# The written-out opening of a two-branch kernel in a new order: an own norm root for each of the first two blocks, the first unit's products block by block

## The chip, the cores and the metric

The kernel runs on one core of one Trainium2 chip. The metric is the device time of one execution in microseconds; lower is better. Before the change it is 443.17 us (median of 3 runs, 442.64 to 443.61).

## The reference

`x` has 2048 rows of 448 numbers. A layer norm is followed by two branches whose results are added to `x`:

```python
xn = _layernorm(x, axis=-1)                      # (x - mean) / sqrt(var + 1e-5)
X  = rfft2(xn, axes=(-2, -1)) * (w_r + 1j * w_i) # spectral branch
a  = irfft2(X, s=(2048, 448))
gate, up = xn @ W_gate, xn @ W_up                # 448 -> 1792
b  = (relu(gate) * up) @ W_down                  # 1792 -> 448
out = x + a + b
```

## The kernel before, in words

Everything stays in one core's memory. Rows of `x` lie in 16 blocks of 128; block n2 belongs to slab q = n2 % 4 at place j = n2 // 4, so a slab is 512 rows. Slabs are worked in the order 0, 2, 1, 3. The 1792 columns of the gate and up weights are 14 tiles f of 128; the two halves of a tile are g0 (gate) and g1 (up). A unit (f, q) is the products of both halves of tile f with slab q. To keep the accuracy of float32, each operand is split into two float16 numbers, hi and lo (the residual); the products are hi x hi, lo x hi and hi x lo. In the code these are three parts of one list: the first three of seq1 (hi weights, hi data), the last three of seq1 (lo weights, hi data), and seq2 (hi weights, and data of the tail tiles, mostly lo).

A block of a slab goes through these steps. SP issues its load (`lx`, load_xr, L225; block 4 comes with the identity for the transposes in one load, L220). VectorE takes its statistics (`st`, ln_stats, L255 and L258). ScalarE takes a first reciprocal root (`sq`, ln_sd, L266) and VectorE improves it by one Newton step (`rs`, ln_rstd, L271 to L275). The normalised block is formed on VectorE (`xn`, L297) or ScalarE (`ax`, L295), its float16 hi on ScalarE (`hi`, `hx`, L304 or L306), two small tail copies on GpSimd (`cp`, L310 and L311), and the residual lo on VectorE (`lo`, ln_lo, L321 and L322). For slab 0 TensorE then transposes the eight tiles (`tpA` the three hi tiles, `tpB` the others, L337), and ScalarE or VectorE copies the result out of PSUM into T (`aev`, `vev`, L345). For the other slabs a transposing DMA does both (`dm`, ln_dma, L330); slab 2's four transfers are the first of these.

A weight half goes: load (`lw`, L231), squares summed on ScalarE (`wsq`, L185), sum over partitions on GpSimd (`par`, L188), a power of two from it on VectorE (`wsc`, L191 and L195), hi on ScalarE (`whi`, L699), lo on VectorE (`wlo`, L703). After a unit, ScalarE and VectorE take turns: `re` (relu, L799), `tm` (gate times up, L803), `gh` (hi, L807), `gl` (lo, L811). `wdq`, `wdp`, `wdsc`, `wdh` and `wdl` prepare the down projection's weights; its products are on L834.

The opening, from the start to the first two units of slab 2, is one string, OPENING. Each word is a piece, and the pieces issue their instructions in the order of the string:

```python
with tc.manual_schedule(engines={PE, DVE, Activation, SP, Pool}):   # names shortened
    A.activation(mt([128, 1], F32, "root"), eps, AF.Abs_reciprocal_sqrt)
    V.memset(warm, 0.0)
    wps = banks[2][0]
    gu_open(0, q)
    for name in OPENING.split():
        pieces[name]()
```

Each engine runs its own instructions strictly in this order; nothing moves an instruction past another of the same engine. So the string sets five rows at once, one for each engine, SP's row of transfers among them. `warm` issues products of a zeroed tile into an unused bank (L1094), `kw4` four more. In the opening, the products of unit (0, slab 0) and (1, slab 0) stand in pieces by half of the slab (256 columns: `hh`, `lh`, `hl` for tile 0, `ah`, `bh`, `ch` for tile 1, followed by the half g and the slab half); later units are whole (`gu`, 512 columns). `hp` is the half-height pass that closes a pair of units (L764). `gz0` and `gz1` are the first two units of slab 2: their first product reads all four blocks of the slab. `n0` gathers the ninth tile of slab 0 by four small transfers. Behind the opening, a scheduler orders the rest of the program.

Of the kernel before, what the change touches and what calls it, by code (L numbers as in the profile page):

```python
# [10 lines left out]
F32 = mybir.dt.float32  # L11
# [3 lines left out]
OP = mybir.AluOpType  # L15
# [10 lines left out]
NWARM = 21  # L26
# [3 lines left out]
OPENING = """lx0 st0 lx4 st4 sqA rsA ax4 hi0 lx8 st8 lx12 xn0 lw cp0 lw lw lw hx4 warm tpA4 st12 tpA0 lo0 lx6 sqB rsB cp4 lo4  # L30
wsqW0g0 tpB0 kw4 tpB4 wsqW0g1 lx2 hi8 parW0g0 wscW0g0 lwd1 whiW0g0 vevA0 parW0g1 wscW0g1 vevA4 hh00 tpA8 whiW0g1
ly4 hi12 lw hh10 lw lw lw wsqW1g1 wsqW1g0 vevB4 vevB0 hl00 wloW0g0 parW1 wloW0g1 tpA12 vevA12 hl10 vevA8 lh00
cp8 xn8 lh10 hh11 lw ax12 lh11 wscW1 whiW1g0 hh01 cp12 whiW1g1 lh01 lw lo8 wsqW2g1 wsqW2g0 tpB8 ah00 lwd0 lo12
tpB12 wsqW3g0 vevB8 wloW1g0 ah10 wsqW3g1 vevB12 ah01 parW2 ah11 lwd2 wloW1g1 wscW2 bh00 hl11 hl01 lx14 whiW2g0
bh01 hp0 ch10 whiW2g1 lw st2 bh11 st6 re0 wloW2g0 bh10 wsqW4g1 ch00 ch11 tm0 gu2g0 parW3 wscW3 st14 wsqW4g0
whiW3g0 wloW2g1 ch01 ly0 parW4 wscW4 whiW3g1 wloW3g1 lw wsqW5g1 lx10 whiW4g0 wloW3g0 gh0 re1 st10 gu2g1 tm1 hp2
sqC rsC wsqW5g0 xn6 gu3g0 re2 parW5 wscW5 whiW5g0 tm2 wloW4g0 xn10 xn14 hx14 lwd4 hx6 lo6 hi10 whiW5g1 lo10
gu4g0 hx2 wloW5g0 whiW4g1 cp14 xn2 wdq0 gl0 cp10 gu3g1 wloW4g1 lo14 lwd3 wdq4 wdq2 cp2 re3 tm3 cp6 wloW5g1 gh1
gu4g1 gh2 wdq3 ly12 lo2 hp4 wdq1 wdp wdsc wdh4 dm10 gl1 re4 ly8 wdh3 gl2 gu5g1 tm4 gh4 dm14 gl4 dm6 gu5g0 dm2
re5 lfd gz0g0 wdl3 gz0g1 tm5 hp6 gh3 gl3 rz0 gh5 wdl4 gl5 wdh1 wdl1 wdh2 wdl2 n0 wdh0 wdl0 gz1g0 tz0 gz1g1 rz1  # L40
hz0 tz1 hz1 lz0 lz1
# [103 lines left out]
def tile_gfnet_reglu(ctx: ExitStack, tc: tile.TileContext, x, xr, xi, wgu, wd, wf, c_fd, c_fm, c_im, c_row, c_id,  # L145
# [106 lines left out]
    def ln_stats(q, j):  # L252
        n2 = q + 4 * j
        st = ft([128, 6], F32, "bst", 2)
        V.bn_stats(st, xr_t[n2])  # L255
        if j == 0:
            mv[q] = ft([128, 4, 2], F32, "mv", 2)
        V.bn_aggr(mv[q][:, j, :], st)  # L258

    rst = {}  # L260

    def ln_sd(q, js=(0, 1, 2, 3)):
        w = ft([128, 4, 4], F32, "rs", 3)
        n = len(js)
        rst[q, js[0]] = w[:, :, 0:n], mv[q][:, js[0]:js[-1] + 1, :]
        A.activation(w[:, 0, 0:n], rst[q, js[0]][1][:, :, 1], AF.Abs_reciprocal_sqrt, bias=eps)  # L266

    def ln_rstd(q, js=(0, 1, 2, 3), bias=False):
        w, m = rst[q, js[0]]
        r0, t, r, nm = (w[:, i] for i in range(4))  # L270
        V.scalar_tensor_tensor(t, m[:, :, 1], 1e-5, r0, op0=OP.add, op1=OP.mult)  # L271
        V.scalar_tensor_tensor(t, t, -0.5 * 2048, r0, op0=OP.mult, op1=OP.mult)
# [17 lines left out]
    def ln_xn(n2, act=False):  # L290
        xn_b[n2] = free.pop(0)
        xn[n2] = xn_b[n2].rearrange("p g c k -> p (g c k)")[:, 0:D]
        r, nm, mean = rst[n2 % 4, n2 // 4]
        if act:
            A.activation(xn[n2], xr_t[n2], AF.Identity, scale=r, bias=nm)  # L295
        else:
            V.tensor_scalar(xn[n2], xr_t[n2], mean, r, op0=OP.subtract, op1=OP.mult)  # L297

    def ln_hi(n2, fused=False):
        new_tt(n2)  # L300
        o = tt[n2].rearrange("p a b -> p (a b)")[:, 0:D]
        r, nm, _ = rst[n2 % 4, n2 // 4]
        if fused:
            A.activation(o, xr_t[n2], AF.Identity, scale=r, bias=nm)  # L304
        else:
            A.activation(o, xn[n2], AF.Copy)  # L306
# [12 lines left out]
    def ln_lo(n2):  # L319
        x, t = xn[n2], tt[n2].rearrange("p a b -> p (a b)")  # L320
        V.tensor_tensor(t[:, 512:896], x[:, 0:384], t[:, 0:384], op=OP.subtract)  # L321
        V.tensor_tensor(t[:, 448:512], x[:, 384:448], t[:, 384:448], op=OP.subtract)  # L322
        free.append(xn_b.pop(n2))
# [373 lines left out]
    def w_hi(f, g):  # L697
        w = wt[f, g] = mt([128, 8, 128], F16, "wt", 2 * NR + 4)
        A.activation(w[:, 0:4, :], wst[f, g], AF.Copy, scale=wsc[f, g])  # L699
# [392 lines left out]
    def keep_warm(n):  # L1092
        for _ in range(n):
# [3 lines left out]
              "lw": load_wn, "warm": lambda: keep_warm(NWARM),  # L1097
              **{f"kw{n}": (lambda n=n: keep_warm(n)) for n in (1, 3, 4)},
# [6 lines left out]
    for c, q in enumerate(CHUNKS[:2]):  # L1105
# [31 lines left out]
    for f in groups[0] + [ahead[2]]:  # L1137
# [149 lines left out]
```

## Time and profile before

| what | value |
|---|---|
| time, median of 3 | 443.17 us |
| profiled execution, span | 440.9 us |
| TensorE (PE) busy | 435.7 us, 99% |
| VectorE (DVE) busy | 382.3 us, 87% |
| ScalarE (ACT) busy | 184.5 us, 42% |
| DMA | 39.55 MB, mean 90 GB/s |

The profile is one profiled execution; its times are microseconds from the start of the span. What lies around the span is the difference to the device time, 443.17 - 440.9 = 2.3 us by the median. A busy TensorE says little, since products overlap in the records; what it waited for, and at what moment, says more. Lines such as L757 are line numbers of the kernel before. In a row of the timeline the columns are start, length, engine, line, operation, what is written and read, shape and count, and in brackets the idle time before it with what ended it.

### The profile page before, as it was taken

The numbers are of one execution on the slowest core, as the hardware profiler recorded it, in microseconds if no ns is written. First come the engines' busy times: TensorE is split into PE (matmuls) and PEld (weight loads), VectorE is DVE, ScalarE is ACT, GpSimd is POOL, SyncE is SP. The second block draws the span as 40 slices with busy tenths as digits, with TensorE's granted clock in tenths as the row PEclk, the third lists the DMA queues.
The fourth block names the chain that finished last, engine by engine and source line by source line (L and its number), as shares of the span: only waits on it lengthen the run. The fifth ranks groups of instructions, "written<-read, shape, count | busy, mean of one in ns | idle before, by whom it ended". The sixth has DMA issues, their size and how long they took to land.

```text
span 440.9 us, 7429 instructions
## 1 busy us (share of the span) xinstructions
PE 435.7 (99%) x2641; PEld 221.9 (50%) x2641; DVE 382.3 (87%) x957; ACT 184.5 (42%) x396; POOL 29.4 (7%) x75
## 2 busy tenths in 40 slices
PE   8999999999999999999999999999999999999996
PEld 3744464554445545444545444444545555555664
DVE  6998496989887879999999999988997989798644
ACT  6995427392457236144023467233113332243220
POOL 3230002011100040000000020000000000000000
PEclk9999999999999999999999999999999999999999
DMA  7929895304111123332220210001111121210212
GB/s 256 301 91 198 269 364 172 70 2 107 59 49 50 47 76 119 94 118 84 86 84 1 84 43 1 0 1 42 44 43 49 54 91 34 72 55 33 89 51 104
DMA packets 37613, 39.55 MB, mean 90 GB/s; under 512 B 16535, under 2 KB 33353, under 8 KB 37577
## 3 DMA queue, kind: packets, MB, share of 16 engines
q1 hardware_dynamic: 37576, 39.09, 29.1%
q8 instruction: 20, 0.33, 0.3%
q14 instruction: 17, 0.13, 0.1%
HBM read 24.38 MB, written 3.67 MB: 64 GB/s over the span
## 4 chain that ended last, share of the span: by engine, by line
PE 90%; DVE 4%; ACT 3%; DMA 1%; issue 1%; SPq 0%; POOL 0%; ACTq 0%
PE bank L757 49%; PE bank L834 27%; PE bank L764 3%; PE fx L648 2%; PE fx L369 2%; PE fx L667 2%; PE fx L406 2%; PE bank L853 2%; ACT wt L699 1%; DMA T<-tt 1%; ACT junk L185 1%; DVE bst L255 1%; DVE wt L703 1%; DMA y<-in_xr 1%; ACT tt L304 1%
## 5 line engine op out<-in xcount | busy, mean ns | idle before, releaser
L757 PE MATMUL bank<-T,wt 128*128 128x512 f16 (+1 forms) x1160 | 252.7, 372 | 0.6 <-DVE T L345 0.5
L757 PEld LDWEIGHTS <-wt 128*128 128x128 f16 x1160 | 110.9, 98 | 127.6 <-issue 7.2
L834 PE MATMUL bank<-wdt,h 128*128 128x448 f16 x624 | 122.4, 352 | 0.0
L834 PEld LDWEIGHTS <-h 128*128 128x128 f16 x624 | 60.5, 98 | 55.1
L799 ACT ACTIVATE g<-bank 128x512 f32<-128x512 f32 x56 | 33.0, 591 | 80.4 <-PE bank L757 45.2
L807 ACT ACTIVATE h<-g 128x512 f16<-128x512 f32 x56 | 35.0, 627 | 70.1 <-DVE g L803 70.0
L803 DVE SCALAR_TENSOR_TENSOR g<-bank,g 128x512 f32<-128x512 f32 x56 | 38.2, 683 | 11.9 <-PE bank L757 6.8
L811 DVE TENSOR_TENSOR h<-g,h 128x512 f16<-128x512 f32 x56 | 38.1, 684 | 6.7 <-ACT h L807 6.4
L840 DVE SCALAR_TENSOR_TENSOR xy<-bank,dsc,xy 128x448 f32<-128x448 f32 x44 | 29.8, 676 | 5.5 <-PE bank L834 5.2
L632 ACT ACTIVATE vt<-y,fsc 128x456 f16<-128x456 f32 x15 | 10.1, 674 | 34.5 <-issue 14.0
L699 ACT ACTIVATE wt<-wst,wsc 128x512 f16<-128x512 f32 x28 | 19.3, 713 | 11.1 <-DVE wsc L195 10.3
L703 DVE SCALAR_TENSOR_TENSOR wt<-wst,wsc,wt 128x512 f16<-128x512 f32 x28 | 20.4, 742 | 0.5 <-ACT wt L699 0.3
L672 DVE SCALAR_TENSOR_TENSOR xy<-fx,fsc,xy 128x448 f32<-128x448 f32 x16 | 10.8, 680 | 10.9 <-PE fx L667 10.9
L188 POOL PARTITION_ALL_REDUCE wm<-wm x15 | 10.5, 697 | 139.9 <-ACT junk L185 136.4
L185 ACT ACTIVATE junk<-wst 128x512 bf16<-128x512 f32 x28 | 17.2, 616 | 0.0
L397 ACT ACTIVATE Xh<-X 128x456 f16<-128x456 f32 x16 | 9.3, 579 | 16.4 <-DVE X L395 9.3
L764 PE MATMUL bank<-T,wt 64*128 64x512 f16 x112 | 15.6, 380 | 0.0
L400 DVE TENSOR_TENSOR Xh<-X,Xh 128x456 f16<-128x456 f32 x16 | 9.8, 624 | 4.9 <-ACT Xh L397 4.9
L648 PE MATMUL fx<-im,vt 128*128 128x128 f16 x192 | 13.3, 219 | 0.0
L667 PEld LDWEIGHTS <-pgh 114*128 114x128 f16 x192 | 10.9, 98 | 3.8 <-issue 0.8
L648 PEld LDWEIGHTS <-vt 128*128 128x128 f16 x192 | 11.6, 98 | 1.3
L406 PE MATMUL fx<-Xh,fm 128*128 128x456 f16 x48 | 12.2, 356 | 0.0
(168 smaller groups left out, 480.1 us busy)
## 6 DMA issues: line engine op xcount, KB each, us to landing
wst<-in_wgu SPq DMA_DIRECT2D x28, 256.0 KB
sw<-y SPq DMA_DIRECT2D x56, 112.2 KB
wf<-in_wf SPq DMA_DIRECT2D x16, 228.0 KB
xy<-in_x SPq DMA_DIRECT2D x16, 224.0 KB
y<-in_xr SPq DMA_DIRECT2D x15, 224.0 KB
out<-xy SPq DMA_DIRECT2D x15, 224.0 KB
wdst<-in_wd SPq DMA_DIRECT2D x14, 224.0 KB
fm<-in_c_fm SPq DMA_DIRECT2D x4, 256.0 KB
```

What stands on the lines that cost most here:

```text
L185: A.activation(mt([128, 512], BF16, "junk", 2)[:, 0:src.shape[-1]], src, AF.Square, scale=SQ, accum_out=acc)
L648: P.matmul(o, v[:, h, w], m[:, c, :], start=(i == 0), stop=(i == 2), skip_group_check=True)
L699: A.activation(w[:, 0:4, :], wst[f, g], AF.Copy, scale=wsc[f, g])
L703: V.scalar_tensor_tensor(w[:, 4:8, :], st, sc, w[:, 0:4, :], op0=OP.mult, op1=OP.subtract)
L757: last["P"] = P.matmul(hps[f, q][g][:, cs], wt[f, g][:, a, :], Tq[q][:, b, cs], start=(start and i == 0), stop=(stop and i == len(seq) - 1 ...
L764: m = P.matmul(hps[f, q][g][:, 0:512], wt[f, g][rows, 7, :], Tq[q][rows, b, :], start=start, stop=stop).ins
L799: last["A"] = A.activation(g1s[f, q], hps[f, q][0], AF.Relu, scale=2.0 ** -22).ins
L803: last["V"] = V.scalar_tensor_tensor(g1, hps[f, q][1], 2.0 ** -22, g1, op0=OP.mult, op1=OP.mult).ins
L807: A.activation(ht[f, q][:, 0, :], g1s[f, q], AF.Copy)
L811: V.tensor_tensor(h[:, 1, :], g1s.pop((f, q)), h[:, 0, :], op=OP.subtract)
L834: last["P"] = P.matmul(ps[:, 0:D], ht[f, q][:, a, js], wdt[f][:, b, :], start=(i == 0), stop=(i == n - 1)).ins
L840: last["V"] = V.scalar_tensor_tensor(xy[:, n2, :], dps[n2][:, 0:D], dsc[:, g:g + 1], xy[:, n2, :], op0=OP.mult, op1=OP.add).ins
```

## The change

OPENING is another string. In words, what it does in the first microseconds: the load of block 4 is issued ahead of that of block 0, both halves of weight tile 0 come third and fourth, and blocks 8 and 12 fifth and eighth. Blocks 4 and 0 each have an own root and an own Newton step (`sq4 rs4`, `sq0 rs0`) instead of one for both; their bias is no longer formed there but later (`nm0`, `nm4`). Block 4 is normalised on VectorE instead of ScalarE. The hi copies of both (`hx4`, `hx0`) come from the normalised block. The warm-up has 14 products instead of 21. Tile 0's products with the first half of slab 0 are split by block: `hq`, `lq` and `kq`, followed by the half g and the block's place j, take 128 columns each. The first group of copies out of PSUM (the hi tiles of blocks 0, 4 and 8) is ScalarE's (`aevA`) instead of VectorE's.

The core of the diff:

```diff
-OPENING = """lx0 st0 lx4 st4 sqA rsA ax4 hi0 lx8 st8 lx12 xn0 lw cp0 lw lw lw hx4 warm tpA4 st12 tpA0 lo0 lx6 sqB rsB cp4 lo4
-wsqW0g0 tpB0 kw4 tpB4 wsqW0g1 lx2 hi8 parW0g0 wscW0g0 lwd1 whiW0g0 vevA0 parW0g1 wscW0g1 vevA4 hh00 tpA8 whiW0g1
...
+OPENING = """lx4 warm14 lx0 st4 lw sq4 st0 wsqW0g0 rs4 lw parW0g0 sq0 lx8 lw wsqW0g1 kw4 xn4 rs0 hx4 wscW0g0 whiW0g0 lw xn0 parW0g1
+hx0 cp4 st8 wscW0g1 wsqW1g0 cp0 tpA0 tpA4 wsqW1g1 aevA0 lx12 lo0 whiW0g1 tpB0 hq00 aevA4 lo4 vevB0 st12 parW1 tpB4
...
     def ln_sd(q, js=(0, 1, 2, 3)):
-        w = ft([128, 4, 4], F32, "rs", 3)
+        w = ft([128, 4, 4], F32, "rs", 4)
...
         if bias:
-            V.scalar_tensor_tensor(nm, m[:, :, 0], -1.0, r, op0=OP.mult, op1=OP.mult)
+            ln_bias(q, js)
...
+    def ln_bias(q, js):
+        w, m = rsb[q, js[0]]
+        V.scalar_tensor_tensor(w[:, 3], m[:, :, 0], -1.0, w[:, 2], op0=OP.mult, op1=OP.mult)
...
+            piece(f"sq{n2}", ln_sd, q, (j,))
+            piece(f"rs{n2}", ln_rstd, q, (j,))
+            piece(f"nm{n2}", ln_bias, q, (j,))
...
             if f == 0:
+                for j in range(2):
+                    for tag, sq in (("hq", seq1[0:3]), ("lq", seq1[3:6]), ("kq", seq2)):
+                        piece(f"{tag}{g}{j}", gu_full, f, q, (g,), slice(128 * j, 128 * j + 128), tag == "hq" and j == 0,
+                              False, sq)
```

Further new pieces (`px`, `ph`, `pl`, `vh`, `pw`, `vw`) move steps to GpSimd or VectorE; the string does not use them.

How rows of engines move, at three places. First SP's row at the start. In it `g1` is block 4 with the identity, the other `y` are blocks of slab 0 or 2 in the order of the string, and `wst` are weight halves. Before:

```order
L225 DMA y0_66<-in_xr 128x448
L220 DMA g1_127<-in_xi 128x512
L225 DMA y2_68<-in_xr 128x448
L225 DMA y3_69<-in_xr 128x448
L231 DMA wst_146<-in_wgu 128x512
L231 DMA wst_150<-in_wgu 128x512
L231 DMA wst_152<-in_wgu 128x512
L231 DMA wst_154<-in_wgu 128x512
```

And now:

```order
L219 DMA g1_122<-in_xi 128x512
L224 DMA y0_66<-in_xr 128x448
L230 DMA wst_143<-in_wgu 128x512
L230 DMA wst_156<-in_wgu 128x512
L224 DMA y1_67<-in_xr 128x448
L230 DMA wst_162<-in_wgu 128x512
L230 DMA wst_180<-in_wgu 128x512
L224 DMA y4_70<-in_xr 128x448
```

Tile 0's two halves moved from the fifth and sixth place to the third and fourth, block 8 from third to fifth, block 12 from fourth to eighth.

Second, VectorE's row from the second but last residual of slab 2 on. `tt` are the blocks in float16: before, tt0 is block 14 and tt3 block 2. Rows that write `g1` are `tm`, those that write `h` are `gl`, those that write `wt` are `wlo`. Before:

```order
L811 TENSOR_TENSOR h_465<-g1_404,h_465 128x512
L703 SCALAR_TENSOR_TENSOR wt_541<-wst_315,wsc_450,wt_541 128x512
L321 TENSOR_TENSOR tt0_100<-y13_79,tt0_100 128x384
L322 TENSOR_TENSOR tt0_100<-y13_79,tt0_100 128x64
L803 SCALAR_TENSOR_TENSOR g1_573<-bank3_114,g1_573 128x512
L703 SCALAR_TENSOR_TENSOR wt_525<-wst_456,wsc_509,wt_525 128x512
L321 TENSOR_TENSOR tt3_103<-y14_80,tt3_103 128x384
L322 TENSOR_TENSOR tt3_103<-y14_80,tt3_103 128x64
```

And now, where tt1 is block 14, tt2 block 6 and tt3 block 10 (block 2, tt0, stands earlier in the row):

```order
L326 TENSOR_TENSOR tt1_101<-y11_77,tt1_101 128x384
L327 TENSOR_TENSOR tt1_101<-y11_77,tt1_101 128x64
L711 SCALAR_TENSOR_TENSOR wt_551<-wst_445,wsc_511,wt_551 128x512
L811 SCALAR_TENSOR_TENSOR g1_610<-bank3_114,g1_610 128x512
L819 TENSOR_TENSOR h_562<-g1_457,h_562 128x512
L326 TENSOR_TENSOR tt2_102<-y14_80,tt2_102 128x384
L327 TENSOR_TENSOR tt2_102<-y14_80,tt2_102 128x64
L326 TENSOR_TENSOR tt3_103<-y13_79,tt3_103 128x384
L327 TENSOR_TENSOR tt3_103<-y13_79,tt3_103 128x64
```

Three residuals of slab 2 instead of two now stand at the end, two of them back to back, and one more `gl` stands ahead of them.

Third, SP's row where slab 2 is transposed, with the same numbers of `tt`. Before:

```order
L214 DMA xy_61<-in_x 128x448
L330 DMA_TRANSPOSE T2_63<-tt2_102 128x8x128
L214 DMA xy_61<-in_x 128x448
L330 DMA_TRANSPOSE T2_63<-tt0_100 128x8x128
L330 DMA_TRANSPOSE T2_63<-tt1_101 128x8x128
L330 DMA_TRANSPOSE T2_63<-tt3_103 128x8x128
L231 DMA wst_750<-in_wgu 128x512
```

And now:

```order
L1104 DMA fd_t_99<-in_c_fd 128x912
L240 DMA wdst_605<-in_wd 128x448
L335 DMA_TRANSPOSE T2_63<-tt1_101 128x8x128
L335 DMA_TRANSPOSE T2_63<-tt2_102 128x8x128
L335 DMA_TRANSPOSE T2_63<-tt0_100 128x8x128
L335 DMA_TRANSPOSE T2_63<-tt3_103 128x8x128
L230 DMA wst_769<-in_wgu 128x512
```

Before, the blocks go in the order 10, 14, 6, 2; now in the order 14, 6, 2, 10, with block 2 third. The four small transfers of `n0` and the load `lfd` moved from behind them to ahead of them. Behind the opening, the scheduler's order of TensorE's row differs up to about the 980th product; there the first two products of the down projection now stand ahead of gz0.

More of the change, by code (lines that the diff above doesn't have):

```diff
@@ L34 @@
[L34 to L38, printed above, removed]
@@ L42 @@
+cp6 xn10 whiW5g1 gh0 lo2 wloW4g0 ly0 cp2 xn6 gh1 lwd2 gu3g1 wdq3 tm2 gl0 gu4g0 wloW5g0 hx10 gu4g1 lfd lo14 lwd1
+wloW5g1 cp14 re3 wdq2 tm3 wdq1 gl1 hp4 lo6 lo10 dm14 gu5g0 cp10 wdp wdsc re4 gh2 dm6 tm4 wdh0 gu5g1 wdh2 gh4 wdh1 gl2
+dm2 re5 dm10 wdh4 tm5 gz0g0 gh3 gh5 wdl1 gl3 wdh3 gz0g1 wdl2 gl4 gl5 wdl0 hp6 rz0 gz1g0 tz0 hz0 gz1g1 lz0 rz1 wdl4 tz1
+hz1 wdl3 lz1
 """
@@ L1151, in tile_gfnet_reglu @@
             piece(f"whiW{f}g{g}", w_hi, f, g)
+            piece(f"pwW{f}g{g}", w_hi, f, g, G)
+            piece(f"vwW{f}g{g}", w_hi, f, g, V)
             piece(f"wloW{f}g{g}", w_lo, f, g)
```

53 lines of the change are left out of this document (29 added, 24 removed).

## The prediction

> **What bounds the kernel now.** I read the page's span first, then what TensorE waited for, then its timeline through the opening, then the chain of waits around the one wait that stands out.
>
> ```profile
> span 440.9 us, 7429 instructions
> ```
>
> All that TensorE's products (PE) waited for over the span, in total, times, longest; and of its weight loads (PEld) the one wait for a transfer:
>
> ```profile
> PE bank L1094 <- DVE row_t L1166: 1.2, 1, 1.2
> PE bank L757 <- DVE T L345: 0.5, 1, 0.5
> ```
> ```profile
> PEld L757 <- DMA T<-tt: 0.6, 1, 0.6
> ```
>
> The first is ahead of the warm-up products, the second ahead of the first real product, and the third ahead of the first product of slab 2. TensorE's timeline (start, length, count; L1094 warm-up, L337 transposes, L757 gate and up products) shows where these stand:
>
> ```profile
> 8.52 0.78 PE L337 MATMUL fx<-g,tt 128*128 128x128 f16 x11
> 9.13 1.03 PE L1094 MATMUL bank<-row_t 128*128 128x512 f16 x4
> 9.99 0.44 PE L337 MATMUL fx<-g,tt 128*128 128x128 f16 x5
> 10.93 0.49 PE L757 MATMUL bank<-T,wt 128*128 128x256 f16 x3 [0.49 <-DVE T L345]
> ...
> 26.41 8.81 PE L757 MATMUL bank<-T,wt 128*128 128x512 f16 x40
> ...
> 35.73 9.09 PE L757 MATMUL bank<-T,wt 128*128 128x512 f16 x40
> ```
>
> The reader is to see that the useful stream begins at 10.93, that 40 products took 8.81 where nothing was late and 9.09 where slab 2 was late (0.28 lost), and, from the waits, that no product waits later on up to the end. So the time is the moment at which the stream starts, plus its fixed work, plus each wait in it. Only two moments of this change can count: when the first product starts, and when the first product of slab 2 (gz0) starts. The chain around the second:
>
> ```profile
> 36.42 3.87 DMA T<-tt
> 40.33 4.49 PE bank L757 x20
> ...
> 168.06 11.35 PE bank L834 x60
> ```
>
> gz0 started at 40.33 because the last of slab 2's four transposing transfers, issued at 36.42, was used 3.87 later. Without it TensorE would have started at 40.33 - 0.28 = 40.05. (The last row gives 11.35 / 60 = 0.19 us for a product of the down projection, used below.)
>
> **The loads in their new order.** The transfers land one after another on shared engines, so a place in SP's queue is a time. Stretches of the span with DMA share and GB/s, and two starts that bound landings:
>
> ```profile
> 3.31:8.13 4.82, 1.00 0.90 263
> 8.13:13.00 4.87, 1.00 1.04 394
> ```
> ```profile
> 3.31 0.63 DVE L255 BATCH_NORM_STATS2 bst<-y 128x6 f32<-128x448 f32 x1 [2.14 <-DMA y<-in_xr]
> ```
> ```profile
> 8.13 0.61 ACT L185 ACTIVATE junk<-wst 128x512 bf16<-128x512 f32 x1
> ```
>
> The first slab block (224 KB) was used at 3.31; after that 263 GB/s. In the new order W0's gate half is third (736 KB in all): 3.31 + 524 kB / 263 = 5.3, taken 5.5. W0's up half is fourth (992 KB): 6.3, taken 6.5. Block 8 is fifth (1216 KB): 7.2, and at the latest about 8.1, since W0's gate half, fifth in the old order, was squared from 8.13; taken 8.1. W1's up half is seventh: 9.2, taken 9.4.
>
> **When the first product starts.** Lengths of one operation each, by shape, in the first 30 us:
>
> ```profile
> L699 ACT ACTIVATE wt<-wst,wsc 128x512 f16<-128x512 f32 x11 | 7.5, 713 | 0.9 <-DVE wsc L195 0.7
> ...
> L306 ACT ACTIVATE tt<-y 128x448 f16<-128x448 f32 x2 | 1.1, 558 | 0.0
> ...
> L297 DVE TENSOR_SCALAR y<-y,mv,rs 128x448 f32<-128x448 f32 x5 | 2.4, 504 | 0.0
> ...
> L345 DVE COPY T<-fx 128x384 f16<-128x384 f16 x3 | 1.0, 348 | 0.0
> ...
> L272 DVE SCALAR_TENSOR_TENSOR rs<-rs 128x2 f32<-128x2 f32 x2 | 0.3, 160 | 0.1
> ```
>
> Operations of one engine overlap a little, as the last residual (lo) of slab 2 before the change shows on VectorE (DVE), whose second part starts 0.08 ahead of the first one's end:
>
> ```profile
> 35.05 0.55 DVE L321 TENSOR_TENSOR tt<-y,tt 128x384 f16<-128x384 f32 x1
> 35.52 0.22 DVE L322 TENSOR_TENSOR tt<-y,tt 128x64 f16<-128x64 f32 x1
> ```
>
> ScalarE (ACT) decides. Its new row is root 4, square of W0's gate half, root 0, square of the up half, then hx4, whiW0g0, hx0, two squares of W1, aevA0. A square costs its 0.61, its short read-out lying in the overlaps. I walk the rows with these lengths. From 6.5: square to 7.15, hx4 to 7.65, whiW0g0 to 8.3, hx0 to 8.8. The first transposes follow at 8.9 instead of 8.52. The squares of W1 wait for 9.4, so aevA0, a copy out of PSUM that ACT did not do in this opening (bounds 0.35 for VectorE's copy above and 0.56 for ACT's 448-wide copy; 0.4 taken, the nearer), runs 10.05 to 10.45. First product: 10.5, against 10.93. The warm-up is not in the way; its weight loads show its pace:
>
> ```profile
> 6.32 0.15 PEld L1094 LDWEIGHTS <-row_t 128*128 128x128 f16 x1 [0.28 <-issue]
> 6.75 1.22 PEld L1094 LDWEIGHTS <-row_t 128*128 128x128 f16 x6 [0.28 <-issue]
> ```
>
> One comes each 0.43 until 6.75, then about twice as often (4 products in 1.03 at 9.13): 14 from 1.2 on and the four after them end by 8.1.
>
> That 0.4 does not last. Block 0's lo copy and block 4's copy vevB4 stand on DVE behind the statistics of blocks 8 and 12 and their loads, so the second block's seq2 products wait about 0.5, and W2's residual, late in DVE's row, costs about 0.3 ahead of gu2g0. Five more transposes are still to do at the first product (11 done instead of 16): 5 x 0.057, from (0.78 - 0.44) / 6, is 0.3. TensorE took 40.05 - 10.93 = 29.1 from the first product to gz0, short waits of its own included. So it reaches gz0's place at 10.5 + 29.1 + 0.3 + 0.8 = 40.7 (bounds 39.6, if the loads run at 394 from the start and the early waits go, and 41.5, if the up half of W0 lands 0.8 later). Two products of the down projection now stand ahead of gz0, 2 x 0.19: 41.1.
>
> Splitting 20 products of 256 columns into 40 of 128 costs almost nothing by these rows: transposes, each with its own weight load, already follow each other 0.057 apart, and 40 x 0.057 is 2.3 against 20 x 0.109. [...]
>
> **When slab 2 is there.** DVE must finish the residuals (lo) of blocks 14, 6 and 10; then SP issues the transfers. DVE's work up to the end of before's last residual, quoted above:
>
> ```profile
> 3.31:35.74 32.43, 30.75 (x89) 1.00 0.69 221
> ```
>
> DVE is packed: 30.75 busy in 32.43. Up to its last residual (now block 10's) the new row holds 92 instructions: three 384-wide copies less (-1.05, they are ACT's now), one 448-wide normalisation more (+0.50), gl1 in front of lo6 (about +0.6, near the residual's 0.55), and four more short root operations (4 x 0.16): +0.7. Waits change too: by the same walk about 0.45 for root 0 behind W0's square, 0.45 for block 8, 0.75 for gl0, whose gh0 comes late in ACT's row; some 1.2 of before's 1.68 go: +0.4. So the last residual ends near 35.74 + 1.1 = 36.8, and block 6's, 0.6 before it, at 36.2 (bounds 35.3 without the two load waits, 37.0).
>
> On SP it is worse than the 1.1. Before, one transfer was left when the last residual ended. Now dm6 stands ahead of dm2, whose block is ready since about 29.6 by the walk, and of dm10: three transfers are still to issue from 36.2. How long that takes, from SP's row for the last four in the trace, and what the DMA engines moved during slab 2's transfers and behind those four:
>
> ```profile
> 99.30 5.47 SPq L330 DMA_TRANSPOSE T<-tt  x4
> ```
> ```profile
> 36.80:37.20 0.40, 1.00 1.83 16
> 37.20:38.00 0.80, 1.00 0.04 6
> ```
> ```profile
> 105.50:106.00 0.50, 1.00 0.56 119
> 106.00:106.30 0.30, 1.00 0.02 3
> ```
>
> Undisturbed, they are issued 1.4 apart (5.47 / 4), and the last, issued at 99.30 + 3 x 1.4 = 103.5, had moved its data by 106.0: 2.5, some 2.7 with its signal. So the last lands at 36.25 + 2 x 1.4 + 2.7 = 41.75, and gz0 starts at 41.8. TensorE, there at 41.1, waits 0.7.
>
> **The sum.** gz0 at 41.8 instead of 40.33 is +1.5; two products already done are -0.4: +1.1. No wait comes after that, so it stays to the end: span 442.0. The profiled execution's 440.9 is 2.3 below the median of 443.17, and the same lies around it: **444.3 us**. A measurement of this kernel tells from no change about 0.2%, 0.9 us.
>
> **Rivals.**
> 1. The transfers stumble as they did in slab 2 of before: from 36.80 to 38.00 the engines moved 16 and 6 GB/s, and the last transfer took 3.87. Then the last of three, issued at 39.05, is used at 42.9: +2.2, 445.4. For it: it happened there; against: in the other row of four it did not. 0.20.
> 2. The loads run faster than 263 GB/s, DVE loses no time early, block 6's residual ends at 35.3, slab 2 lands at 40.9: +0.2, 443.4, no difference. For it: the rate is 394 from 8.13 on, and nothing shows what held the earlier one. 0.25.
> 3. Faster: the early start carries through. With fast loads and only 0.6 of the 0.8 of short waits TensorE reaches gz0 at 39.4 + 0.4 = 39.8: -0.9, 442.3. It decides from the point where slab 2 is there by then, its last transfer issued by 37.1 and so block 6's residual done by 34.3. Against: that is 1.9 us less DVE work in a row of 30.75. 0.06.
> 4. The array's clock, by the warm-up's two paces above. If, with 14 warm-up products and gaps of up to 0.8 between 8.1 and 10.5, the array fell back to half pace for some 3.4 us, 1.7 of work would be lost, of which 0.7 hides in the wait at gz0: +2.1, 445.3. [...] 0.05.
>
> **How the numbers follow.** The forecast has 0.44. The range 443.1 to 445.8 holds it, rivals 2, 4 and most of 1, and leaves out rival 3 and the end of 1. Slower by over 0.9: 0.40 of the forecast, 0.20 and 0.05: 0.65. Within 0.9: rival 2, the rest of the forecast and a little of rival 3: 0.30. Faster: 0.05.
>
> **What would show it.** Right: aevA0 ends near 10.5 and the first product follows; block 6's residual ends near 36.2; SP's last three transposes issue 1.4 apart from there; TensorE's weight load waits for T<-tt some 0.7 near 41; then no wait. Wrong: no such wait and gz0 before 40; first products at half pace; or a new wait of TensorE later, where the scheduler interleaves the transform's products in another order.

## The result, and the profile after

After: **447.98 us** (median of 4 runs, 447.67 to 449.31); before, on the same chip, 443.01 us (442.64 to 443.61). Ratio 1.0112, interval 1.0094 to 1.0131: slower by 5.0 us, where I had forecast 1.1 (444.3, at most 445.8).

The profiled execution of after is the longest of the four (449.31). Its span is 6.6 us longer than before's 440.9; around the span lie 449.31 - 447.5 = 1.8 us, not the 2.3 that I had added:

```profile
span 447.5 us, 7454 instructions
```

What TensorE's products (PE) waited for over the span: total, times, longest.

```profile
PE bank L765 <- DMA T<-tt: 3.3, 2, 2.3
PE fx L342 <- ACT tt L311: 2.3, 1, 2.3
PE fx L342 <- ACT T L348: 1.3, 2, 1.1
```

The first row holds two waits for transposing transfers; I had forecast one of 0.7. Here is TensorE's timeline (L1102 warm-up, L342 transposes, L765 products, L772 the half-height pass hp, L842 down products, L374 and L411 products of the transforms):

```profile
5.79 0.81 PE L1102 MATMUL bank<-row_t 128*128 128x512 f16 x3
8.89 0.51 PE L342 MATMUL fx<-g,tt 128*128 128x128 f16 x6 [2.29 <-ACT tt L311]
10.49 0.48 PE L342 MATMUL fx<-g,tt 128*128 128x128 f16 x5 [1.09 <-ACT T L348]
10.77 0.53 PE L765 MATMUL bank<-T,wt 128*128 128x128 f16 x3
...
27.95 0.61 PE L772 MATMUL bank<-T,wt 64*128 64x512 f16 x4
...
37.23 0.61 PE L772 MATMUL bank<-T,wt 64*128 64x512 f16 x4
37.77 4.49 PE L765 MATMUL bank<-T,wt 128*128 128x512 f16 x20
42.10 0.54 PE L842 MATMUL bank<-wdt,h 128*128 128x448 f16 x2
43.59 4.48 PE L765 MATMUL bank<-T,wt 128*128 128x512 f16 x20 [0.96 <-DMA T<-tt]
...
82.94 0.21 PE L374 MATMUL fx<-fd_t,Tl 128*128 128x114 f16 x1
85.48 6.16 PE L765 MATMUL bank<-T,wt 128*128 128x512 f16 x20 [2.33 <-DMA T<-tt]
```

The first product starts at 10.77 (before 10.93). hp2 comes at 27.95 and hp4 at 37.23, where before had 25.87 and 35.19: 2.0 late. Slab 2's first product (gz0) follows a wait of 0.96 and starts at 43.59, 3.26 after before's 40.33. Then, 42 us further on, stands a wait of 2.33 that before does not have: the first product of slab 1, the third slab. The 20 products behind it take 6.16, where 20 such products took 4.49 at 37.77. The clock is the reason. Here are two stretches of the span, with their length, the busy time of each engine and, third from the end, the granted clock (the share of its full speed that TensorE was given):

```profile
10.77:14.10 3.33, 3.15 (x32) 2.98 (x30) 2.85 (x11) 2.39 (x6) 0.00 (x0) 0.50 0.58 223
85.48:89.00 3.52, 3.52 (x10) 1.30 (x11) 3.52 (x11) 0.00 (x0) 0.00 (x0) 0.55 0.16 54
```

Twice TensorE ran at half its clock for over 3 us: at the first products, and behind the wait at slab 1. The span's 6.6 us are therefore about: gz0 3.26, less 0.38 for the two down products done ahead of it, 2.33 at slab 1, and 6.16 - 4.49 = 1.67 for the half pace behind it. That makes 6.9, and where the 0.3 too much goes is not shown. The median run is shorter by 1.3: a half-paced stretch of 3.4 us takes 0.5 x 3.4 / 447 = 0.004 off the mean clock of the span, which is 0.992 here and 0.995 or 0.996 in the three other runs (447.67 to 448.23), so they had one such stretch and not two; which one, their results do not say.

What holds slab 1 back is read on VectorE (DVE) and SP:

```profile
59.12 0.68 DVE L848 SCALAR_TENSOR_TENSOR xy<-bank,dsc,xy 128x448 f32<-128x448 f32 x1 [3.90 <-PE bank L842]
59.73 1.14 DVE L254 BATCH_NORM_STATS2 bst<-y 128x6 f32<-128x448 f32 x2
```
```profile
75.72 2.69 SPq L335 DMA_TRANSPOSE T<-tt  x2
78.52 1.70 SPq L563 DMA_DIRECT2D row<-y  x2
80.39 3.47 SPq L335 DMA_TRANSPOSE T<-tt  x2
```

and in before:

```profile
55.19 0.68 DVE L840 SCALAR_TENSOR_TENSOR xy<-bank,dsc,xy 128x448 f32<-128x448 f32 x1 [3.22 <-PE bank L834]
```
```profile
73.13 5.51 SPq L330 DMA_TRANSPOSE T<-tt  x4
```
```profile
81.72 3.62 PE L757 MATMUL bank<-T,wt 128*128 128x512 f16 x16
```

In both kernels VectorE stands idle for over 3 us at the first copy of the down products, with slab 1's statistics right behind it. That copy came 3.93 later (59.12 against 55.19). ScalarE (ACT) then waits 3.47 for slab 1's root and normalises the slab from 71.02 on (66.85 in before), the first residual follows at 74.86 (71.70), and the last transpose is issued at 82.63 (77.3). TensorE was at slab 1 only 1.4 later (82.94 + 0.21 = 83.15 against 81.72), since the scheduler had put other products behind slab 1. So slab 1's preparation, just in time before, was late.

### The profile page after: what moved, and what is told of

Same layout as the page of the kernel before. It is cut to its first block, busy times and chain, and to the rows that moved or that the text cites. A ratio compares the mean times of both kernels' runs of the same rounds, so it can differ in the third digit from the quotient of the medians.

```text
span 447.5 us, 7454 instructions
## 1 busy us (share of the span) xinstructions
PE 436.3 (97%) x2654; PEld 223.0 (50%) x2654; DVE 382.2 (85%) x959; ACT 184.8 (41%) x399; POOL 31.1 (7%) x75
## 4 chain that ended last, share of the span: by engine, by line
PE 80%; DMA 6%; DVE 5%; ACT 4%; SPq 2%; issue 1%; POOL 0%; ACTq 0%; DVEq 0%
PE bank L765 44%; PE bank L842 24%; PE bank L772 3%; PE fx L653 2%; DMA y<-in_xr 2%; PE fx L672 2%; DMA wst<-in_wgu 2%; PE bank L861 2%; PE fx L411 2%; PE fx L374 2%; DMA xy<-in_x 1%; ACT junk L184 1%; ACT tt L309 1%; SPq L335 1%; SPq L230 1%
## 5 line engine op out<-in xcount | busy, mean ns | idle before, releaser
L765 PE MATMUL bank<-T,wt 128*128 128x512 f16 (+2 forms) x1180 | 255.8, 372 | 3.4 <-DMA T<-tt 3.3
L765 PEld LDWEIGHTS <-wt 128*128 128x128 f16 x1180 | 113.0, 99 | 131.5 <-issue 13.4
L842 PE MATMUL bank<-wdt,h 128*128 128x448 f16 x624 | 122.6, 352 | 0.0
L842 PEld LDWEIGHTS <-h 128*128 128x128 f16 x624 | 60.6, 98 | 55.3
L848 DVE SCALAR_TENSOR_TENSOR xy<-bank,dsc,xy 128x448 f32<-128x448 f32 x44 | 29.8, 678 | 7.0 <-PE bank L842 6.7
L772 PE MATMUL bank<-T,wt 64*128 64x512 f16 x112 | 15.6, 380 | 0.0
L411 PE MATMUL fx<-Xh,fm 128*128 128x456 f16 x48 | 12.5, 356 | 0.0
L672 PE MATMUL fx<-idc_t,pgh 114*128 114x112 f16 x192 | 12.1, 213 | 0.0
```

Of the source, the lines that this page charges most:

```text
L411: P.matmul(y, m[:, a, :], xh[:, b], start=(i == 0), stop=(i == 2), skip_group_check=True)
L672: P.matmul(ps[:, o], h[:, a, i, :], idc_t[:, b, o], start=(j == 0), stop=(j == 2), skip_group_check=True)
L765: last["P"] = P.matmul(hps[f, q][g][:, cs], wt[f, g][:, a, :], Tq[q][:, b, cs], start=(start and i == 0), stop=(stop and i == len(seq) - 1 ...
L772: m = P.matmul(hps[f, q][g][:, 0:512], wt[f, g][rows, 7, :], Tq[q][rows, b, :], start=start, stop=stop).ins
L842: last["P"] = P.matmul(ps[:, 0:D], ht[f, q][:, a, js], wdt[f][:, b, :], start=(i == 0), stop=(i == n - 1)).ins
L848: last["V"] = V.scalar_tensor_tensor(xy[:, n2, :], dps[n2][:, 0:D], dsc[:, g:g + 1], xy[:, n2, :], op0=OP.mult, op1=OP.add).ins
```

## The experiments

Each was timed beside before on the same chip; before's medians there were 442.98 to 443.40, so that differences between experiments of different rounds are sure to some 0.4 only. First I took three losses for independent: the half pace, slab 2's transfers, and the two row transfers between slab 1's transposes on SP.

### x_clock: after, TensorE kept busy ahead of the first product

```diff
-... wsqW0g1 kw4 xn4 ... tpA4 wsqW1g1 aevA0 ...
+... wsqW0g1 kw14 xn4 ... tpA4 kw4 wsqW1g1 aevA0 ...
```

> After, with 14 warm-up products instead of 4 behind the first 14, and 4 more between the transposes tpA4 and tpB0: TensorE's two idle stretches of 2.29 and 1.09 us ahead of the first product are filled, nothing else moves. Theory: the products from 10.8 to 14.1 run at full pace again (a pitch of 0.056 for 128 columns instead of 0.107), hp0 comes 1.5 to 1.8 us earlier, near 20.1; but slab 2's transfers are set by VectorE and SP, so gz0 still starts at 43.0 to 43.6 and TensorE waits 2 to 2.7 us there instead of 0.96, perhaps with a half-paced stretch behind that wait. The time: 446.5 to 449, hardly better than after's 447.98. Rival 1, the half-paced first products are the loss and nothing stands behind them: 446.2 or less, gz0 near 41.9. Rival 2, the clock does not depend on these gaps: the half-paced stretch stays, no change.

Measured 450.25 us, ratio 1.0153 (1.0133 to 1.0174): worse than after. The first products ran at full pace, but the filling ended late and pushed the transposes back; the first product came at 11.83:

```profile
5.47 4.48 PE L1102 MATMUL bank<-row_t 128*128 128x512 f16 x18
9.96 0.51 PE L342 MATMUL fx<-g,tt 128*128 128x128 f16 x6
...
11.83 0.33 PE L765 MATMUL bank<-T,wt 128*128 128x128 f16 x3
```

hp0, expected near 20.1, came at 21.98, and W2's first products now waited 0.62 and 1.02. gz0 did not come earlier (45.41), and the wait at slab 1 was 2.27, with a half-paced stretch behind it. So with the first products at full pace another bound, W2, stood behind them; the theory had that in kind, and underestimated the cost of the filling. What the half pace alone costs the run does not show, since the filling also moved the first product by 1.06.

### x_slab2: after, slab 2's residuals and transposes earlier

```diff
-... lo14 lwd1 wloW5g1 cp14 re3 wdq2 tm3 wdq1 gl1 hp4 lo6 lo10 dm14 gu5g0 cp10 ... dm6 ... dm2 re5 dm10 ...
+... lo14 lwd1 cp14 cp10 lo6 lo10 dm2 dm14 dm6 dm10 wloW5g1 re3 wdq2 tm3 wdq1 gl1 hp4 gu5g0 ...
```

> After, with the residuals of blocks 6 and 10 ahead of W5's second residual, gl1 and their like, and slab 2's four transposes in the order in which the blocks are ready (2, 14, 6, 10). Theory: the last transfer lands near 41.0 instead of 43.46, TensorE no longer waits at gz0 (0.96 gone), and the two down products fall behind gz0 (0.38 earlier, no gain): gz0 near 42.2 to 42.6, the time 1.0 less than after, 447.0 (446.5 to 447.5). The half-paced first products and the wait at slab 1 stay. Rival: the order of the transfers does not matter since VectorE only pays elsewhere (gl1 later): no change, 448.

447.59 us, ratio 1.0103 (1.0089 to 1.0117): 0.4 gained instead of 1.0. The wait at gz0 went, but part of it came back at hp4, whose bank waits for tm3, now behind the two residuals:

```profile
38.79 0.61 PE L772 MATMUL bank<-T,wt 64*128 64x512 f16 x4 [0.73 <-DVE g L811]
```

The wait at slab 1 was 1.53 in this profile, without a half-paced stretch behind it.

### x_rows: after, slab 0's row transfers behind slab 1's transposes

```diff
-            last["R"] = nc.sync.dma_start(row[...], ...)
+            with tc.high_priority(offset=-100 if j in (0, 4) else 0):
+                last["R"] = nc.sync.dma_start(row[...], ...)
```

> After, with the four row transfers of slab 0 at a lower priority, so that SP issues them behind slab 1's four transposes; the rows of the other engines are as they were. Theory: slab 1's last transpose is issued near 80.4 instead of 82.4, TensorE's wait of 2.33 at 83 goes to 0 to 0.3, and the half-paced stretch behind it (85.5 to 89, 1.6 lost) goes with it: 2.3 to 3.9 less than after, 444.1 to 445.7. Rival, all of the loss arises in the opening and slab 1 only shows it, or the residuals on VectorE and not SP's row set that wait: 447 or more, the wait stays above 1.5.

448.38 us, ratio 1.0112 (1.0096 to 1.0127): nothing gained.

```profile
76.76 2.69 SPq L335 DMA_TRANSPOSE T<-tt  x2
...
80.26 3.58 SPq L335 DMA_TRANSPOSE T<-tt  x2
83.89 3.28 SPq L564 DMA_DIRECT2D row<-y  x4
```
```profile
86.14 6.16 PE L766 MATMUL bank<-T,wt 128*128 128x512 f16 x20 [1.97 <-DMA T<-tt]
```

The row transfers are behind, and the wait is 1.97 all the same. But the chain of waits shows that the last transpose was issued earlier, at 81.66 instead of 82.63, although its residual ended later (80.65 instead of 79.63), and that it then took 4.35 instead of 2.71 (before's slab 2 had one of 3.87). Here is its row, and the same in after:

```profile
81.66 4.35 DMA T<-tt
```
```profile
82.63 2.71 DMA T<-tt
```

With 2.71 it would have been there at 84.37, 0.2 behind TensorE, which came to slab 1 at 86.14 - 1.97 = 84.17. So this profile, of the longest of the five runs (450.13), does not refute the part of my theory that named SP's row; a slow transfer hid it. The median says that nothing was gained, and why the other runs gained nothing is open.

### x_all: the three edits together

> After with all three edits: warm-up products in the gaps, slab 2's residuals and transposes earlier, slab 0's row transfers behind slab 1's transposes. Theory, the three losses add up and are all of it: first products at full pace, no wait at gz0 (near 40.5), none at slab 1: 442.8 (442.2 to 443.6), the same as before's 443.0 within 0.2%. Rival, something else of the change costs as well (the split into 128 columns, the later copies): 444.5 or more.

447.64 us, ratio 1.01 (1.0084 to 1.0116): far from 442.8. With the first products at full pace a new wait stood at W2's first products, as in x_clock: VectorE had waited 2.06 for the load of a block, and W2's residual stands behind it:

```profile
23.24 0.63 DVE L254 BATCH_NORM_STATS2 bst<-y 128x6 f32<-128x448 f32 x1 [2.06 <-DMA y<-in_xr]
```
```profile
25.06 5.96 PE L766 MATMUL bank<-T,wt 128*128 128x512 f16 x19 [1.49 <-DVE wt L712]
```

The theory of three independent losses falls. The new one: in the opening several bounds lie one behind another, and slab 1 hangs on the copy of the down products.

### y_ah6 and y_ah6b: slab 1 prepared earlier, in after and in before

AHEAD is the number of units by which the work for a slab is given to the scheduler ahead of its first product.

```diff
-LAG, AHEAD, RAMP = 1, 5, 8
+LAG, AHEAD, RAMP = 1, 6, 8
```

> After, with AHEAD = 6 instead of 5: slab 1's statistics, root, residuals and transposes are given to the scheduler one unit earlier, so that on VectorE they stand ahead of the first down products' copy (L848), for which VectorE waited 3.90 in after, and SP issues the four transposes together. The opening is word for word after's. Theory now: slab 1's preparation hangs on that copy, so the wait of 2.33 at slab 1's first product, and any half-paced stretch behind it, go: 2.3 to 3.9 less than after, 444.9 (444.0 to 445.7). Rival, the wait only moves to a later transfer or to the down products, whose copies now stand behind slab 1's preparation: 447 or more.

445.86 us, ratio 1.0056 (1.0041 to 1.007): 2.1 less than after, or 2.5 by the distance of each to the before beside it. The theory's upper end counted the half-paced stretch behind the wait too; by the mean clock only the profiled one of after's runs had both such stretches. Slab 1's statistics stand ahead of the copy, and its four transposes are issued together from 69.43, where after issued the last pair at 80.39:

```profile
54.97 1.15 DVE L254 BATCH_NORM_STATS2 bst<-y 128x6 f32<-128x448 f32 x2
...
59.74 0.68 DVE L848 SCALAR_TENSOR_TENSOR xy<-bank,dsc,xy 128x448 f32<-128x448 f32 x1 [0.42 <-PE bank L842]
```
```profile
69.43 6.43 SPq L335 DMA_TRANSPOSE T<-tt  x4
```

No product waits at slab 1 any more.

> Before, with AHEAD = 6 instead of 5, as the control. Theory: before has no wait at slab 1 (its last transpose lands 1.6 us ahead of TensorE), so nothing is to be gained: 443.0, within 0.4. Rival, the earlier preparation is a gain by itself, whatever the opening: 442 or less.

444.80 us, ratio 1.0036 (1.0023 to 1.0049): in before the same number costs 1.4 us. TensorE's waits from 90 us on in this kernel's profile, of which before has none:

```profile
PE bank L764 <- DVE g L803: 2.5, 4, 1.2
```

Neither theory had that; it is clear at least that AHEAD = 6 is no gain by itself. What it mends in after is after's own lateness.

### y_op2 and y_all2: W2 ahead of the late loads, with x_slab2's order

```diff
-... lx14 wsqW4g1 lh01 ... whiW2g0 parW4 hl01 wscW3 whiW2g1 lw hp0 lwd3 re0 st14 wscW4 ... re1 wloW2g0 ...
+... lx14 lh01 ... whiW2g0 hl01 wscW3 whiW2g1 wsqW4g1 parW4 lw hp0 lwd3 re0 wloW2g0 st14 wscW4 ... re1 ...
```

> After, with slab 2's residuals and transposes earlier (as in x_slab2), and W2 ahead of two things that wait for late loads: on ScalarE the square of W4's up half behind W2's hi copies instead of ahead of them, on VectorE W2's first residual ahead of the statistics of block 14. Theory: in the opening TensorE loses its time at W2's first products (gu2g0), which wait for W2 behind those two loads, so that a half-paced stretch before is hidden: hp2 comes at 27.0 to 27.8 instead of 28.7 in x_slab2, and the time is 0.5 to 1.5 less than x_slab2's 447.59: 446.6. Rival, the start of the first products and their half pace set the opening: hp2 and the time as in x_slab2.

447.08 us, ratio 1.0081 (1.0069 to 1.0094). hp2 came at 27.95 (28.72 in x_slab2), in spite of half-paced first products, but hp4 waited 1.26 instead of 0.73 and had only 0.23 of the 0.77 left:

```profile
27.95 0.61 PE L772 MATMUL bank<-T,wt 64*128 64x512 f16 x4
...
38.56 0.61 PE L772 MATMUL bank<-T,wt 64*128 64x512 f16 x4 [1.26 <-DVE g L811]
```

VectorE could not follow.

> After with AHEAD = 6 and both edits of the opening. Theory: the losses at W2, at slab 2 and at slab 1 add up and are all of it: 443.6 (443.0 to 444.4), 0.2 to 1 above before at most. Rival, one of them only moves: 445 or more.

With AHEAD = 6 as well: 445.60 us, ratio 1.0049 (1.0034 to 1.0063), 2 more than expected: hp4 waits 1.26 here too, and W2's first products wait 0.83 and 0.29.

### z_loads and z_lw2: two block loads ahead of the ninth weight load

SP's row in after: nothing is issued between 7.79 and 14.38, because the next weight load needs the buffer of W0, which VectorE frees with W0's residual (in the row of 13.55), and everything behind waits with it, the loads of blocks 2 and 14 too.

```profile
7.79 0.33 SPq L224 DMA_DIRECT2D y<-in_xr  x1
14.38 0.33 SPq L230 DMA_DIRECT2D wst<-in_wgu  x1
```
```profile
13.55 2.07 DVE L711 SCALAR_TENSOR_TENSOR wt<-wst,wsc,wt 128x512 f16<-128x512 f32 x3
```

z_loads is y_ah6 with this edit; z_lw2 has y_op2's edit for W2 as well:

```diff
-... lx10 wloW1g0 ... wloW1g1 lx2 ly12 ... vevB8 lx14 ...
+... lx10 lx2 lx14 wloW1g0 ... wloW1g1 ly12 ... vevB8 ...
```

> y_ah6 (after with AHEAD = 6), with the loads of blocks 2 and 14 ahead of the ninth weight load in SP's row. That load waits for W0's gate buffer, which W0's residual frees on VectorE near 14.3, so that from 13.4 to 16.3 nothing lands and block 14 comes at 22 to 23. Theory: block 14 lands near 14.7, VectorE no longer waits for it (0.9 to 1.6 in the runs without half-paced products), slab 2's residuals end as much earlier and gz0 with them: 0.5 to 1.1 less than y_ah6's 445.86: 445.0 (444.7 to 445.4). Rival: VectorE is held by the copies of TensorE's transposes and W2's hi, the loads only fill time that is lost anyway: 445.6 to 446.1.

445.40 us, ratio 1.0051 (1.0038 to 1.0064): 0.5 less than y_ah6's, at the edge of what the theory gave, and 0.2 less by the distances to before. The intervals overlap, so a gain is not shown. VectorE no longer waits for blocks 2 and 14.

> z_loads, and W2 ahead of the late loads as in y_op2 (square of W4's up half behind W2's hi copies, W2's first residual ahead of block 14's statistics). Theory: hp2 comes near 27 instead of 28.2, but the first product of slab 2 is set by VectorE and SP, so TensorE waits longer there: as z_loads within 0.4, 444.9. Rival: TensorE's own time in the opening counts, then 0.8 or more less than z_loads.

445.98 us, ratio 1.0057 (1.0042 to 1.0073): 1.1 more than expected, and 0.6 more than z_loads, though the intervals overlap. Of six runs, two had a mean granted clock of 1.0 and took 444.65 and 444.89; four had 0.996 and took 445.89 to 446.39. In y_ah6 there was no such difference (445.61 to 446.32 at 0.999 and 1.0, 445.55 to 446.13 at 0.996). So with the bounds behind it removed the half pace seems to count; w_fill tests it.

### w_fill, w_fill2 and w_whole: what is left of the opening

w_fill is z_lw2 with more warm-up products, fewer than in x_clock:

```diff
-... wsqW0g1 kw4 xn4 ... tpA4 wsqW1g1 aevA0 ...
+... wsqW0g1 kw10 xn4 ... tpA4 kw4 wsqW1g1 aevA0 ...
```

w_fill2 adds slab 2's order, with the residuals behind tm3 this time and not ahead of it:

```diff
-... lo14 lwd1 wloW5g1 cp14 re3 wdq2 tm3 wdq1 gl1 hp4 lo6 lo10 dm14 gu5g0 cp10 ... dm6 ... dm2 re5 dm10 ...
+... lo14 lwd1 cp14 cp10 dm2 dm14 wloW5g1 re3 wdq2 tm3 lo6 lo10 dm6 dm10 wdq1 gl1 hp4 gu5g0 ...
```

> z_lw2 with TensorE kept busy: 10 warm-up products instead of 4 behind the first 14, and 4 between tpA4 and tpB0. z_lw2's runs fall into two groups by their mean clock, 444.65 and 444.89 at 1.0 against 445.9 to 446.4 at 0.996. Theory: with the loads and W2 out of the way the half-paced first products do count, 1.3, and they come from the idle stretches ahead of them; filled, all runs lie with the first group: 444.7 (444.4 to 445.1), mean clock 0.999 to 1.0. Rival: the slower group has another cause (slow loads) that also lowers the clock: two groups again, the median near 446.

445.31 us, ratio 1.006 (1.0046 to 1.0075). The mean clock is 0.999 or 1.0 in all six runs, so the idle stretches are the cause of the half pace, as the theory says. But the runs spread from 444.84 to 446.63, the median is 0.6 above the theory's, and the wait of 1.4 at gz0 is still there. Two runs (446.30, 446.63) are as slow as z_lw2's slower group at a full clock. In the profiled one (446.63) W0's up half was squared from 7.71 on, 6.90 in w_fill2's profile, and the first transposes came at 10.03 instead of 9.23. So late loads can give such a time as well, and how much of z_lw2's difference is the clock's is not shown.

> w_fill with slab 2's residuals of blocks 6 and 10 one place earlier on VectorE (ahead of gl1, behind tm3) and its four transposes issued in the order 2, 14, 6, 10. Theory: what is left of the opening's loss is the wait of 1.3 to 1.4 at slab 2's first product, since three transposes are still to issue when block 6's residual is done; with two to issue, and 0.6 earlier, it shrinks to 0.3 or less: 443.7 (443.3 to 444.2). Rival: VectorE only pays at hp4 or later, as in y_op2: 444.5 or more.

443.74 us, ratio 1.0015 (1.0002 to 1.0028): 1.6 less, as expected. From the first product to the end of slab 2's first units no product waits:

```profile
36.58 0.61 PE L772 MATMUL bank<-T,wt 64*128 64x512 f16 x4
37.12 8.82 PE L765 MATMUL bank<-T,wt 128*128 128x512 f16 x40
45.77 0.54 PE L842 MATMUL bank<-wdt,h 128*128 128x448 f16 x2
```

Slab 1 is in time too, and from 90 us on no product waits, so that AHEAD = 6 does not cost here what it cost in before (y_ah6b). This is after with all the waits mended that I found, and it is still 0.8 behind before. The rest lies in the opening: the first product stands at 11.10 here and at 10.93 there, hp4 at 36.58 and at 35.19.

w_whole is w_fill2 with the first unit's products of both blocks together:

```diff
-... hq00 ... kq00 hq10 ... kq10 hq11 ... hq01 ... kq01 lw kq11 ... lq00 ... lq10 ... lq11 ... lq01 ...
+... hh00 ... hh10 ... hl00 lw hl10 ... lh10 ... lh00 ...
```

> w_fill2 with the first unit's products of both blocks together, 256 columns each, 20 fewer products, instead of block by block. Theory: the split costs nothing (0.056 for 128 columns against 0.109 for 256), but without it the first product waits for the second block's copies: later by 0.4 to 0.7 at the first products, and 0 to 0.4 in the time: 443.9 (443.6 to 444.3). [...]

444.26 us, ratio 1.0037 (1.0023 to 1.0052), 0.5 above w_fill2, though the intervals overlap. No cost of the split into blocks is seen, and it may gain some.

### z_roots and b_warm14: one part alone, in before

```diff
-lx0 st0 lx4 st4 sqA rsA ax4 hi0 ...
+lx0 st0 sq0 lx4 rs0 nm0 st4 sq4 rs4 nm4 ax4 hi0 ...
```

> Before with one part of the change alone: an own root and an own Newton step for blocks 0 and 4 (four more short operations of 0.16 on VectorE), the rest of the opening word for word. Theory: before's first product waits for W0 and not for the norm, so the earlier norm of block 0 gives nothing, and 0.6 more on a packed VectorE reaches slab 2 and costs at most that: 443.2 to 444.0. Rival, the own roots are the good part of the change and start the stream earlier: 442.6 or less.

The string is before's with these pieces, run in after's code. 444.06 us, ratio 1.0023 (1.001 to 1.0036): 0.9 lost, a little more than the top of the theory's range. The four short operations count, but not as work at the end of a packed row: block 0's root and Newton step stand ahead of block 4's statistics, where VectorE waits 0.36 for ScalarE and works 0.66 on the four, so that these statistics start at 5.25 instead of 4.07. Block 4's norm on ScalarE in this kernel:

```profile
7.22 0.76 ACT L298 ACTIVATE y<-g,rs 128x448 f32<-128x448 f32 x1 [0.81 <-DVE rs L280]
```

and in before:

```profile
6.02 0.76 ACT L295 ACTIVATE y<-g,rs 128x448 f32<-128x448 f32 x1 [0.81 <-DVE rs L275]
```

W0's squares stand behind it in the row, and the first product moved from 10.93 to 12.13.

> Before with 14 warm-up products instead of 21, nothing else. TensorE is then idle for 1.3 to 3.3 us ahead of its transposes at 8.52, four more warm-up products follow at 9.13. Theory: an idle stretch of some 2 us takes the clock down (after and x_rows fell to half pace with 2.2 to 2.3, y_ah6 did not with 1.3), and the first products run at half pace for 1 to 2 us: 443.7 to 444.5. [...]

`NWARM = 14` in before: 442.87 us, ratio 0.9993 (0.9985 to 1.0002), no difference, and no half pace. But the case was not tested: the warm-up ended at 7.21, and TensorE was idle for 0.83 and 0.56 only, or for 2.19 up to the next warm-up products at 9.40, if the transposes between count as idle.

```profile
1.22 5.99 PE L1094 MATMUL bank<-row_t 128*128 128x512 f16 x14 [1.22 <-DVE row_t L1166]
8.04 0.51 PE L337 MATMUL fx<-g,tt 128*128 128x128 f16 x6 [0.83 <-ACT tt L306]
```

## Why the prediction was wrong

The direction was right, the size not: +1.1 forecast, +5.0 measured.

- **"No wait comes after that, so it stays to the end."** This step failed, and it is the largest. I had looked for waits of before and found none; I had not looked for how close the others came. Before's last transpose for slab 1 was issued near 73.13 + 3 x 1.38 = 77.3 and, at 2.7 from issue to landing, was there some 1.7 us ahead of TensorE. Slab 1's statistics stood behind a copy that waits for down products, so the late opening, with TensorE's other order behind it, shifted them by the 3.93 of that copy, while the scheduler brought slab 1's first product nearer. In after the wait there was 2.33, and y_ah6 takes 2.1 to 2.5 us away by that alone, more than half of the 3.9 by which the forecast fell short. I had named "a new wait of TensorE later" among the signs of a wrong forecast and given it neither a price nor a chance.
- **The loads and the first product.** Forecast: W0's halves at 5.5 and 6.5, first product at 10.5. The copy aevA0 ran from 9.97 to 10.44 (forecast 10.05 to 10.45), and the product started at 10.77. Right but for 0.27: block 0's five other transposes came between.
- **"The warm-up is not in the way", and rival 4 (0.05).** By its weight loads the warm-up doubled its pace at 3.8 instead of 6.75 (one each 0.43 up to 3.76, then 11 in 2.34), so it ended at 6.60 instead of 8.1. The gaps behind it were 2.29 and 1.09, not up to 0.8, and the first products ran at a granted clock of 0.50. The mechanism of rival 4 came, with a chance that was far too small. No row of before shows the 3.4 us that its price was worked out from; each of after's two half-paced stretches lasted 3.41. Its price I had right in kind: in y_ah6 the runs with and without it take the same time, so there it is hidden.
- **TensorE at gz0's place: 41.1.** It came there at 43.59 - 0.96 = 42.63. From 10.77 that is 31.9, where 29.1 + 0.3 + 0.4 = 29.8 was free of new losses: 2.1 instead of the 0.8 for "short waits". The half pace is at most 0.5 x 3.4 = 1.7 of it; y_op2 suggests that W2 behind the late loads has a part, but how the 2.1 divides is not shown.
- **VectorE's row: +0.7 of work, +0.4 of waits.** The work was nearly right: 31.22 busy against 30.75, so +0.5. The waits were not: 35.09 - 31.22 = 3.87 against 1.68 before, so +2.2.

```profile
3.42:38.51 35.09, 31.41 (x222) 18.80 (x221) 31.22 (x92) 29.30 (x70) 9.23 (x24) 0.95 0.64 207
```

Block 6's residual ended at 37.9 instead of 36.2. Two waits of 0.8 that I had not counted are VectorE's copies of the transposes (L350), which wait for transposes that TensorE does late, one of them behind ScalarE's share of the copies.
- **Three transposes behind block 6's residual.** Right: issued 37.98, 39.25 and 40.73, the last one used 2.9 later, a wait of 0.96 (forecast 0.7). That the wait came out so near is luck: slab 2 came 1.8 and TensorE 1.5 later than forecast. w_fill2 shows what that order costs where nothing else does: 1.6 us with the place of the residuals.
- **The split into 128 columns costs almost nothing.** Right, as far as w_whole shows: without it the time is no shorter (444.26 against 443.74).

The parts by the experiments, each a difference of distances to the before beside it (after 4.97, y_ah6 2.46, w_fill 2.33, w_fill2 0.76): slab 1 2.5 (after to y_ah6), the half pace, loads and W2 together 0.1 (y_ah6 to w_fill), slab 2's order 1.6 (w_fill to w_fill2), and 0.8 that is left. By the bare medians the first two are 2.1 and 0.55; the 1.6 was measured within one round. So a gain of the half pace, loads and W2 is not told from nothing: z_loads, z_lw2 and w_fill differ by little more than their spread. What gave the last 0.8 is not shown either; w_fill2's first product is 0.2 later than before's, TensorE has five more transposes (0.3) to do behind it, and hp4 is 1.4 later.

## What to carry to other kernels

Where a prediction says "no wait behind this point", ask how much time each later transfer has in hand, and whether its preparation hangs on something that the change moves: a stage that is just in time shows no wait and has no room. And a wait that one edit removes was mostly hiding another; x_clock, x_slab2 and y_op2 removed one or two and gained nothing, 0.4 and 0.9, and only the edits together came back to within 0.8 of before.

## What the runs showed of the hardware

TensorE's clock fell to half (0.50 in after) after idle stretches that I had thought harmless. In the opening, taking the transposes as idle, the stretch from the last warm-up product to the first real one was 10.77 - 6.60 = 4.17 us in after. In y_op2 the clock fell after 10.53 - 7.01 = 3.52, and in y_ah6 it held through 11.10 - 7.91 = 3.19:

```profile
3.76 3.25 PE L1102 MATMUL bank<-row_t 128*128 128x512 f16 x12
```
```profile
3.76 4.15 PE L1102 MATMUL bank<-row_t 128*128 128x512 f16 x12
```

(the end of the warm-up in y_op2 and in y_ah6). By these three lengths alone the bound would lie between 3.19 and 3.52. Slab 1 does not agree with that: there the clock fell after waits of 2.33 (after), 2.27 (x_clock) and 1.97 (x_rows), and held through the 1.82 of x_all and the 1.63 of y_op2, whose 20 products took 4.48:

```profile
85.00 4.48 PE L765 MATMUL bank<-T,wt 128*128 128x512 f16 x20 [1.63 <-DMA T<-tt]
```

In x_all it had fallen at W2 after waits of 0.47 and 1.49 with one product between them, and not at once, but at 26.15, 1.09 after work had begun again at 25.06; the 19 products there took 5.96. So the length of a wait does not decide.

The warm-up's products start at 1.22 in before and at 1.23 in after, and the full clock is recorded from 6.82 on in before and from 3.92 on in after. In after each half-paced stretch lasts 3.41 us, from 10.75 to 14.16 and from 85.84 to 89.26, and the two begin 75.09 apart, or 22 x 3.413. I divided the spans of before and after into stretches of 3.413, from the moment at which the full clock begins. The three falls lie on this grid: 10.75 and 85.84 are 2 and 24 stretches behind 3.92, and 440.31, where the clock falls at the end of before's work, is 127 behind 6.82. Behind the stretches in which TensorE was busy for 0.65 us (before, from 436.90 on), 0.77 and 1.08 (after, from 7.34 and 82.43 on), its transposes counted, the clock fell for the next stretch; behind all others that end within the two spans, with 2.45 or more, it held. Here are three rows, each of the stretch just ahead of such a moment (PE's busy time stands behind the length): the opening of after and W2 in x_all, where it fell, and slab 1 in x_all, where it held:

```profile
7.34:10.75 3.41, 0.77 (x11) 0.69 (x12) 2.49 (x9) 3.41 (x9) 2.02 (x6) 1.00 0.99 339
```
```profile
22.74:26.15 3.41, 1.46 (x6) 0.51 (x6) 2.80 (x8) 2.18 (x5) 0.00 (x0) 1.00 0.83 274
84.18:87.59 3.41, 1.59 (x18) 1.02 (x16) 3.41 (x8) 0.88 (x2) 0.00 (x0) 1.00 0.62 124
```

So here the stretch need not be idle, and a wait can cost 1.7 us (the 1.97 of x_rows, 20 products in 6.16) or nothing (the 1.63 of y_op2, 20 in 4.48). That its place on the grid decides is my estimate from these few cases, and whether transposes count as work for the clock is not shown. The ends of products are modelled in the records, so the busy times are those of these profiles.
